# A fixed order on every engine for blocks 1 to 5 of the first layer, instead of one chosen by a scheduler

## The chip, the cores and the metric

The kernel runs on one core of a Trainium2 chip, in one launch. The metric is the device time of that launch in microseconds (us); lower is better. The profile is one further execution of the same program, taken by the hardware profiler.

The engines are named as the profile names them: PE (TensorE, matmuls; PEld is its weight load), DVE (VectorE), ACT (ScalarE), SP (SyncE, which here only issues DMAs). Each engine takes its instructions in its own written order and waits on semaphores for the others.

## The reference, cut to what matters

Attention over chunks of 32 queries, then two feed-forward layers on 3072 tokens of width 512, each with a hidden width of 2048:

```
for c in range(24):                       # chunk of 32 queries, local keys + 8 memory keys
    scores = scale * q_c @ k_full.T       # 64 keys per chunk
    a = exp(scores - max);  a = a / (sum(a) + 1e-9)
    out[c] = a @ v_full
x = out.transpose(0, 2, 1, 3).reshape(3072, 512)
h = relu(x @ w_in);  x = (h * h) @ w_out            # first layer
h = x @ w2_in;       x = softplus(h) @ w2_out       # second layer
```

## The kernel before, in words

**Blocks and steps.** The first layer goes over the tokens in 6 blocks of 512 (`NB`), and in each block over 16 slices of the hidden width (`f`, `KF`). One slice of one block is a step: `h_mm` makes the slice of the hidden product in a PSUM bank `hp` (12 matmuls), `act1` on ACT applies relu, square and a rounding copy `gh`, `act1_low` on DVE subtracts to get the low half `gl`, and `out_mm` (12 matmuls: low weights by `gh`, high weights by `gh`, high weights by `gl`, for each of the four accumulators `acc0` to `acc3`) adds the slice's share to the block's output. Every product is split into high and low halves so that fp32r matmuls give fp32 accuracy. `out_mm` of a slice runs two steps after its `h_mm` (`LOOK`), and at `f == 0` of the next block the last two are worked off; then `evac` copies the four accumulators to tiles `ev` (even ones on ACT, odd ones on DVE) and stores each to `x2s` in DRAM. `ev` and the relu result `r` share one ring of three buffers (tag `tmp`).

**Attention beside it.** While block n runs, attention for block n+1 is made in four pairs, one each four steps: `p_scores` (64 small matmuls), `p_exp` (on DVE maximum and subtraction, on ACT the exponential), `p_norm` (on DVE sum, reciprocal, multiplication), `p_squares` (16 DVE transposes of 32x32 squares into `pt`), `p_values` (64 small matmuls), `p_out` (two ACT copies to `xf`). At the end of a block `x_split` splits `xf` into `xh` (ACT) and `xl` (DVE). The last block, n = 5, has no attention left.

**Weight preparation.** The second layer's weights arrive as 64-bit floats. Pieces of work (`jobs2`) load them to `cf` tiles, join them to fp32 (`r_conv`: one ACT pass, three DVE passes), form sums (a Strassen-like scheme for the second layer), split them into halves (`halves`: an ACT copy, then a DVE subtraction) and store them to `wa`, `wb`, `wo`. About one piece is written into each step.

**What sets the order.** Block 0 stands in the written order on all engines. From `step(1, 0)` on, PE and SP keep the written order and a scheduler places the instructions of ACT and DVE by its own simulated times. Each engine then keeps that order on the chip, whatever the real times are.

Of the kernel before, what the change touches and what calls it, by code (L numbers as in the profile page):

```python
# [55 lines left out]
def body(ctx: ExitStack, tc: tile.TileContext, qk, vW, w1, w2, out):  # L56
# [132 lines left out]
        p_t[n] = t  # L189


    def p_squares(n):
        t = p_t.pop(n).rearrange("p (a i) (h k) -> p i h a k", i=2, h=2)
        pt = at.tile([P, UC * 2, 2 * PU, CHUNK], F32, tag="pt", name="pt", bufs=1)
        for i in range(2):
            for h in range(2):
                b = (2 * i + h) * 32
                for g in range(UC * 2):
                    nc.vector.transpose(pt[b:b + 32, g], t[g * 32:(g + 1) * 32, i, h])  # L199
        pt_t[n] = pt.rearrange("k (c r) (j u) q -> k c r j u q", c=UC, j=2)  # L200

# [153 lines left out]
    def g_step(n, f, hp, cols=ALL):  # L355
        pending.append((n, f, act1(hp, cols), cols))
# [13 lines left out]
    def store(out, in_):  # L370
        nc.sync.dma_start(out=out.bitcast(F32), in_=in_.bitcast(F32))

    def r_load(k, f, part):
        t = cf_tile(k, (P, DM), I64)
        nc.sync.dma_start(out=t, in_=w2[f][:, part * DM:(part + 1) * DM])
        v = t.bitcast(U32).rearrange("p (n t) -> p n t", t=2)
        return v[:, :, 1], v[:, :, 0]

    def r_conv(f, top, low):
        nc.scalar.activation(out=f, in_=top.bitcast(F32), func=AF.Abs, scale=2.0**-112)  # L380
        nc.vector.tensor_scalar(low, low, 2.0**-29, 7.0, op0=ALU.mult, op1=ALU.min)
        f = f.bitcast(U32)
# [7 lines left out]
    def halves(hi, lo, x):  # L390
        nc.scalar.copy(out=hi, in_=x)  # L391
        nc.vector.tensor_tensor(out=lo, in0=x, in1=hi.bitcast(F32), op=ALU.subtract)  # L392

    def in_jobs(p):
        k0, k1, k2 = 0, 1, 2
        d = {}

        def load(i):
            d["r", i] = r_load((k0, k1)[i], 2 * p + i, 0)

        def conv(i):
            if i == 0:
                d["f"] = cf_tile(k2)
            r_conv(d["f"][:, i], *d["r", i])

        def sums():
            f = d["f"].rearrange("p i (h q) -> p i h q", h=2)
            s = d["s"] = cf_tile(k0, (P, 4, QW))
# [7 lines left out]
            store(wb[p][:, 0:2], split(k1, f[:, :, 1]))  # L416
            t = f[:, 1].bitcast(F32R)
            halves(t[:, 0], t[:, 1], f[:, 0, 0])
            store(wa[p][:, 0], t)

        def split(k, x):
            t = cf_tile(k, (P, 2, 2, QW), F32R)
            halves(t[:, :, 0], t[:, :, 1], x)
            return t

        def last():
            t = split(k1, d["s"][:, 0:2])
            u = split(k2, d["s"][:, 2:4])
            store(wa[p][:, 1:3], t)
            store(wa[p][:, 3:4], u[:, 0:1])  # L430
            store(wb[p][:, 2:3], u[:, 1:2])

        return lambda: load(0), lambda: load(1), lambda: conv(0), lambda: conv(1), sums, last

    def out_jobs(f):
        d = {}

        def load():
            d["r"] = r_load(f % 2, f, 1)

        def conv():
            x = cf_tile(2, (P, DM))
            r_conv(x, *d["r"])
            t = cf_tile(f % 2, (P, 2, DM), F32R)
            halves(t[:, 0], t[:, 1], x)
            store(wo[f // 2][:, f % 2], t)

        return load, conv

    ij, oj = [in_jobs(p) for p in range(KP)], [out_jobs(f) for f in range(KF)]  # L450
    jobs2 = [(0, [ij[0][0], ij[0][1]])]
    for p in range(KP):
        after = ij[p + 1][0:2] if p + 1 < KP else (oj[0][0], oj[1][0])
        jobs2 += [(1, [ij[p][2]]), (1, [ij[p][3]]), (1, [ij[p][4]]), (0, [ij[p][5], after[0]]), (0, [after[1]])]
    for f in range(KF):
        jobs2.append((1, [oj[f][1]]))
        jobs2.append((-1, [oj[f + 2][0]] if f + 2 < KF else []))


    xo = {}  # L460
# [7 lines left out]
    def x_jobs(grp, k):  # L468
        d = {}

        def sums(i):
            b11, b12, b21, b22 = (xf_t[2, grp, k][:, j // 2, j % 2] for j in range(4))
            if i == 0:
                if grp == 0:
                    t = late[0].tile([P, 4, BLK], F32, tag="r2", name="xs")
                    d["t"] = t[:, 0], t[:, 1], t[:, 2]
                else:
                    d["t"] = [tmp("xs") for _ in range(3)]
            t3, t2, t4 = d["t"]
            if i == 0:  # L480
                todo = (t3, b22, b12), (b12, b12, b11)
            else:
                todo = (t2, b22, b12), (t4, b21, t2)
            for o, a, b in todo:
                nc.vector.tensor_tensor(out=o, in0=a, in1=b, op=ALU.subtract)
            d["x"] = b11, b12, t2, b22, b21, t3, t4

        def split(i):
            if k == 0:
                xo[grp, i] = wpool.tile([P, 2, 2, BLK], F32R, tag=f"w{i}", name=f"xo{i}")  # L490
            t = xo[grp, i]
            halves(t[:, 0, k], t[:, 1, k], d["x"][i])

        return [lambda: sums(0), lambda: sums(1)] + [lambda i=i: split(i) for i in range(7)]


    with tc.manual_schedule(engines={mybir.EngineType.SP}):
# [134 lines left out]
        def step(n, f):  # L632
            if f == 0:
                out_step()
            hp = h_mm(1, n, f)
            pair = (n + 1) * PB + f // 4 if n < NB - 1 else -1
            if pair >= 0 and f % 4 == 0:
                if f == 0:
                    p_scores(pair)
                p_exp(pair)  # L640
                later_loads(pair)
            if n == NB - 1 and f == 0:
                at_ctx.__exit__(None, None, None)
                pb_ctx.__exit__(None, None, None)
                pl.append(ctx.enter_context(tc.tile_pool(name="pl", bufs=2, space=bass.MemoryType.PSUM)))
                late.append(ctx.enter_context(tc.tile_pool(name="late", bufs=1)))
            g_step(n, f, hp)
            act1_low()
            if pair >= 0 and f % 4 == 0:
                p_norm(pair)  # L650
                p_squares(pair)
            if jobs2 and not (jobs2[0][0] == 1 and pair >= 0 and f % 4 == 0):
                for job in jobs2.pop(0)[1]:
                    job()
            while jobs2 and jobs2[0][0] == -1 and (n == NB - 1 or f % 2):
                for job in jobs2.pop(0)[1]:
                    job()
# [9 lines left out]
            if f == KF - 1 and n < NB - 1:  # L667
                x_split((1, n + 1))
            if f == 0:
                out_step()  # L670
            while len(pending) > LOOK:
                out_step()
            if pair >= 0 and f in (3, 7, 11, KF - 2):
                (p_values if f == KF - 2 else p_both)(pair)
                p_out(pair)
# [141 lines left out]
                xq.setdefault(f, []).extend(j[:n])  # L817
                j = j[n:]

        with tc.manual_schedule(engines={mybir.EngineType.PE}):  # L820
            for n in range(1, NB):
                for f in range(KF):
                    step(n, f)
            assert not jobs2
            for _ in range(3):
                fetch()
            while pending:
                out_step()
            fetch()
            for grp in range(NGR):  # L830
                second_stage(grp, first_stage(grp))

# [44 lines left out]
```

## Time and profile before

| | |
|---|---|
| runs, median (lowest to highest) | 1137.39 us (1135.9 to 1139.78), 3 runs |
| profiled execution | 1138.33 us, span 1136.6 us |
| PE busy | 1091.1 us, 96% of the span |
| DVE busy | 754.5 us, 66% |
| ACT busy | 586.0 us, 52% |
| mean granted TensorE clock | 0.989 of 2.4 GHz |

The span is the time from the program's first to its last instruction; 1.7 us of the execution's time lie outside it. PE is the engine whose work fills the span, so what counts is the time in which it stands idle or runs at a lower clock; busy time of DVE and ACT counts only where PE waits for it.

### The profile page before, as it was taken

Reading aid. Unit: us, or ns where it says so; the run is one execution under the profiler, and the core shown is the slowest. Engines: PE = TensorE matmul, PEld = TensorE weight load, DVE = VectorE, ACT = ScalarE, POOL = GpSimd, SP = SyncE. Lnnn points to the kernel's source line nnn. Section 1 sums busy time; section 2 is a strip of 40 time slices with the busy share of each in tenths; the row PEclk is TensorE's granted clock in tenths of the full one; section 3 lists DMA queues with packets and bytes.
Section 4 is the critical chain, followed back from the end, with each engine's and each line's share of the span. In section 5 each row is a group of like instructions: output and inputs, shape, how many; then the busy total and the mean of one; then the engine's idle time right before and its main releaser. Section 6 shows DMA issues by size and latency. Waiting matters only on the chain.

```text
span 1136.6 us, 18578 instructions
## 1 busy us (share of the span) xinstructions
PE 1091.1 (96%) x7592; PEld 892.8 (79%) x7592; DVE 754.5 (66%) x1239; ACT 586.0 (52%) x914; POOL 0.7 (0%) x6
## 2 busy tenths in 40 slices
PE   6899989999999899998999999999999999999998
PEld 5668868878888687877887878788888888788887
DVE  6899567656665675766364399954498963599822
ACT  3666534435444434444455477733476742576622
POOL 0000000000000000000000000000000000000000
PEclk9999989999999999999999999999999999999999
DMA  9941154435236234632363555532655432656201
GB/s 367 400 161 45 55 162 151 145 125 175 74 125 217 78 138 143 203 113 93 107 236 93 174 187 204 185 137 75 228 192 212 157 108 97 229 192 219 83 1 74
DMA packets 49428, 174.99 MB, mean 154 GB/s; under 512 B 5312, under 2 KB 5312, under 8 KB 41152
## 3 DMA queue, kind: packets, MB, share of 16 engines
q1 hardware_dynamic: 49344, 173.82, 44.0%
q8 instruction: 59, 0.97, 0.4%
q14 instruction: 25, 0.20, 0.1%
HBM read 138.15 MB, written 35.65 MB: 153 GB/s over the span
## 4 chain that ended last, share of the span: by engine, by line
PE 74%; DVE 10%; DMA 10%; ACT 3%; issue 2%; SPq 1%; DVEq 0%; ACTq 0%
PE bk L799 23%; PE bk L711 18%; PE acc L324 15%; PE hp L288 5%; PE hp L289 5%; PE hp L290 5%; DMA cf<-w 4%; DVE pt L199 3%; DMA wo<-cf 2%; DMA wb<-cf 1%; DMA out<-cf 1%; DMA x2s<-ev 1%; DVE cf L392 1%; PE xs L233 1%; DVE cf L110 1%
## 5 line engine op out<-in xcount | busy, mean ns | idle before, releaser
L324 PE MATMUL acc<-gh,w 128*128 128x512 f32 (+1 forms) x776 | 240.5, 392 | 7.0 <-DVE ev L333 6.4
L799 PE MATMUL bk<-ws,gh 128*128 128x512 f32 x768 | 236.5, 389 | 0.0
L711 PE MATMUL bk<-xo,ws 128*128 128x512 f32 x1008 | 230.5, 390 | 2.5 <-ACT h L750 1.3
L711 PEld LDWEIGHTS bk<-xo,ws 128*128 128x128 f32 x1008 | 188.9, 188 | 43.2 <-ACT h L750 2.1
L324 PEld LDWEIGHTS acc<-gh,w 128*128 128x128 f32 x776 | 144.5, 189 | 37.9 <-DVE ev L333 7.3
L799 PEld LDWEIGHTS bk<-ws,gh 128*128 128x128 f32 x768 | 144.1, 188 | 30.0 <-ACT h L731 0.2
L288 PE MATMUL hp<-xh,w 128*128 128x512 f32 (+1 forms) x388 | 156.6, 404 | 9.8 <-ACT r L300 5.3
L324 PE MATMUL acc<-gl,w 128*128 128x512 f32 (+1 forms) x388 | 152.0, 392 | 7.7 <-DVE gl L309 7.6
L289 PE MATMUL hp<-xl,w 128*128 128x512 f32 (+1 forms) x388 | 153.9, 397 | 0.3 <-DVE xl L264 0.2
L290 PE MATMUL hp<-xh,w 128*128 128x512 f32 (+1 forms) x388 | 153.3, 395 | 0.0
L799 PE MATMUL bk<-ws,gl 128*128 128x512 f32 x384 | 149.5, 389 | 0.0
L392 DVE TENSOR_TENSOR gl<-h,gh 128x512 fp32r<-128x512 f32 x96 | 65.9, 688 | 84.4 <-ACT gh L391 84.1
L391 ACT CAST gh<-h 128x512 fp32r<-128x512 f32 x96 | 59.4, 622 | 112.7 <-PE bk L799 112.3
L309 DVE TENSOR_TENSOR gl<-r,gh 128x512 fp32r<-128x512 f32 (+1 forms) x97 | 65.7, 683 | 57.3 <-ACT gh L303 56.9
L300 ACT ACTIVATE r<-hp 128x512 f32<-128x512 f32 (+1 forms) x97 | 57.0, 588 | 86.9 <-PE hp L290 77.6
L288 PEld LDWEIGHTS hp<-xh,w 128*128 128x128 f32 x388 | 75.2, 194 | 27.6 <-ACT r L300 6.1
L324 PEld LDWEIGHTS acc<-gl,w 128*128 128x128 f32 x388 | 73.3, 189 | 25.7 <-DVE gl L309 10.8
L289 PEld LDWEIGHTS hp<-xl,w 128*128 128x128 f32 x388 | 75.2, 194 | 15.8 <-DVE xl L264 0.5
L290 PEld LDWEIGHTS hp<-xh,w 128*128 128x128 f32 x388 | 75.1, 194 | 15.8
L799 PEld LDWEIGHTS bk<-ws,gl 128*128 128x128 f32 x384 | 72.1, 188 | 14.9
L199 DVE STREAM_TRANSPOSE pt<-t 32x128 f32<-32x128 f32 x256 | 77.5, 303 | 3.7
L717 ACT ACTIVATE cf<-h 128x1024 f32<-128x1024 f32 x48 | 51.0, 1062 | 27.6 <-DVE cf L721 20.1
(82 smaller groups left out, 1145.0 us busy)
## 6 DMA issues: line engine op xcount, KB each, us to landing
ws<-wa SPq DMA_DIRECT2D x24, 1024.0 KB, 4.8
ws<-wo SPq DMA_DIRECT2D x24, 1024.0 KB, 4.8
ws<-wb SPq DMA_DIRECT2D x24, 768.0 KB, 4.2
r<-w SPq DMA_DIRECT2D x16, 1024.0 KB, 11.1
cf<-w SPq DMA_DIRECT2D x32, 512.0 KB, 4.6
qk<-qk SPq DMA_DIRECT2D x46, 336.0 KB, 4.8
v<-vW SPq DMA_DIRECT2D x44, 256.0 KB, 4.4
wo<-cf SPq DMA_DIRECT2D x16, 512.0 KB, 4.4
```

Of the source, the lines that this page charges most:

```text
L199: nc.vector.transpose(pt[b:b + 32, g], t[g * 32:(g + 1) * 32, i, h])
L288: nc.tensor.matmul(out=hp, lhsT=b, rhs=xh[:, c], start=(c == 0), stop=False)
L289: nc.tensor.matmul(out=hp, lhsT=a, rhs=xl[:, c], start=False, stop=False)
L290: nc.tensor.matmul(out=hp, lhsT=a, rhs=xh[:, c], start=False, stop=(c == KD - 1))
L300: nc.scalar.activation(out=r, in_=hp, func=AF.Relu)
L309: nc.vector.tensor_tensor(out=gl, in0=r, in1=gh.bitcast(F32), op=ALU.subtract)
L324: nc.tensor.matmul(out=acc[m][:, cols], lhsT=a, rhs=b, start=(f == 0 and j == 0 and cols.start == 0), stop=(f == KF - 1 and j == 2),)
L391: nc.scalar.copy(out=hi, in_=x)
L392: nc.vector.tensor_tensor(out=lo, in0=x, in1=hi.bitcast(F32), op=ALU.subtract)
L711: nc.tensor.matmul(out=bk, lhsT=a, rhs=b, start=(start and n == 0), stop=(n == 5), skip_group_check=not start)
L717: nc.scalar.activation(out=z, in_=h, func=AF.Abs)
L799: nc.tensor.matmul(out=bk, lhsT=a, rhs=b, start=(f == 0 and j == 0), stop=(f == KF - 1 and j == 2))
```

## The change

From `step(1, 0)` to the end of the first layer all engines keep the written order; the second layer is left as it was (PE and SP written, ACT and DVE by the scheduler). Inside `step` the order is written anew:

- First the low half of the step before (`act1_low`) and the low halves that the pieces left over (`flush`), then `h_mm`.
- Then the loads and ACT's first pass (`starts`) of one piece of weight preparation.
- Then, at every fourth step, the softmax with the first 8 of its 16 transposes; the other 8 stand in the next step. At `f == 0` the softmax stands behind relu and `p_scores`.
- Then relu, square and copy, and at the step's end the piece's DVE work and its splits, whose low halves and stores wait for the next step's `flush`.
- `x_split` stands before the relu of step 15 instead of behind it.
- A piece is now one load, one join, one set of sums or one set of splits, and it is skipped only at `f % 8 == 0`.

```
-    def r_conv(f, top, low):
+    def r_abs(f, top, low):
         nc.scalar.activation(out=f, in_=top.bitcast(F32), func=AF.Abs, scale=2.0**-112)
+
+    def r_join(f, top, low):
+        f = f.bitcast(U32)
         nc.vector.tensor_scalar(low, low, 2.0**-29, 7.0, op0=ALU.mult, op1=ALU.min)
...
+    lows = []
+
+    def low_half(hi, lo, x, *stores):
+        nc.vector.tensor_tensor(out=lo, in0=x, in1=hi.bitcast(F32), op=ALU.subtract)
+        for o, i in stores:
+            store(o, i)
+
+    def halves(hi, lo, x, *stores, late=False):
         nc.scalar.copy(out=hi, in_=x)
-        nc.vector.tensor_tensor(out=lo, in0=x, in1=hi.bitcast(F32), op=ALU.subtract)
+        if late:
+            lows.append(lambda: low_half(hi, lo, x, *stores))
+        else:
+            low_half(hi, lo, x, *stores)
+
+    def flush():
+        while lows:
+            lows.pop(0)()
...
+        return [
+            (False, [at(load, 0)], [], []),
+            (True, [at(load, 1)], [at(start, 0)], [at(join, 0)]),
+            (True, [], [at(start, 1)], [at(join, 1)]),
+            (True, [], [], [sums]),
+            (True, [], [], [last]),
+        ]
...
+    jobs2 = [j for p in range(KP) for j in in_jobs(p)]
+    for f in range(0, KF, 2):
+        a, b = out_jobs(f), out_jobs(f + 1)
+        jobs2 += [(False, [a[0]], [], []), (True, [b[0]], [a[1]], [a[2]]), (True, [], [b[1]], [b[2]])]
...
         def step(n, f):
             if f == 0:
                 out_step()
+            if rest:
+                act1_low()
+            flush()
             hp = h_mm(1, n, f)
+
             pair = (n + 1) * PB + f // 4 if n < NB - 1 else -1
-            if pair >= 0 and f % 4 == 0:
-                if f == 0:
-                    p_scores(pair)
+            work = ()
+            if jobs2 and not (jobs2[0][0] and pair >= 0 and f % 8 == 0):
+                _, loads, starts, work = jobs2.pop(0)
+                for job in (*loads, *starts):
+                    job()
+
+            def softmax():
                 p_exp(pair)
                 later_loads(pair)
+                p_norm(pair)
+                p_squares(pair, 0)
+
+            if pair >= 0 and f % 4 == 0 and f > 0:
+                softmax()
...
+            if f == KF - 1 and n < NB - 1:
+                x_split((1, n + 1))
             g_step(n, f, hp)
-            act1_low()
-            if pair >= 0 and f % 4 == 0:
-                p_norm(pair)
-                p_squares(pair)
...
+            if pair >= 0 and f == 0:
+                p_scores(pair)
+                softmax()
+            if pair >= 0 and f % 4 == 1:
+                p_squares(pair, 1)
+            for job in work:
+                job()
...
-        with tc.manual_schedule(engines={mybir.EngineType.PE}):
+        with tc.manual_schedule():
             for n in range(1, NB):
                 for f in range(KF):
                     step(n, f)
             assert not jobs2
+            act1_low()
+            flush()
...
+        with tc.manual_schedule(engines={mybir.EngineType.PE}):
             for grp in range(NGR):
                 second_stage(grp, first_stage(grp))
```

**Place one: DVE in the first step of block 1.** Before, from the low half `gl` of step (1, 0) to the copy of accumulator 3 (`acc_698`; `acc_696` is accumulator 1, `sc`, `t`, `s` and `pt` are the softmax, `cf` the weight preparation):

```order
L309 TENSOR_TENSOR gl<-r,gh 128x512
L177 TENSOR_TENSOR t<-sc,m 128x512
L333 COPY ev<-acc_696 128x512
L185 TENSOR_REDUCE s<-t 128x8
L186 TENSOR_SCALAR s<-s 128x8
L187 RECIPROCAL s<-s 128x8
L188 TENSOR_TENSOR t<-t,s 128x512
L381 TENSOR_SCALAR cf<-cf 128x512
L199 STREAM_TRANSPOSE pt<-t 32x128 x16
L383 SCALAR_TENSOR_TENSOR cf<-cf 128x512
L381 TENSOR_SCALAR cf<-cf 128x512
L333 COPY ev<-acc_698 128x512
```

In the change, the same stretch of DVE, with the semaphores that each row waits for (DMAHW is the landing of a DMA; the one of the second `ev` row is the store of the first):

```order
L177 TENSOR_TENSOR t<-sc,m 128x512 [waits DVE_49]
L185 TENSOR_REDUCE s<-t 128x8 [waits Activation_49]
L186 TENSOR_SCALAR s<-s 128x8 [waits DVE_49]
L187 RECIPROCAL s<-s 128x8 [waits DVE_49]
L188 TENSOR_TENSOR t<-t,s 128x512 [waits DVE_49]
L202 STREAM_TRANSPOSE pt<-t 32x128 [waits DVE_49]
L202 STREAM_TRANSPOSE pt<-t 32x128 x7
L337 COPY ev<-acc_696 128x512 [waits PE_49]
L337 COPY ev<-acc_698 128x512 [waits DMAHW4_49,DVE_49,PE_49]
L313 TENSOR_TENSOR gl<-r,gh 128x512
L202 STREAM_TRANSPOSE pt<-t 32x128 x8
L388 TENSOR_SCALAR cf<-cf 128x512 [waits DMAHW6_49]
```

The low half `gl` of step (1, 0) moved from ahead of the softmax's subtraction to behind both `ev` copies, the first `ev` copy moved behind 8 transposes, and half of the transposes moved behind all of them. Since `gl` comes later, its `r` holds one of the three `tmp` buffers, and the second DVE copy takes the buffer of the first one. The rows in the first steps of blocks 2, 3 and 4 stand the same way.

**Place two: ACT in steps 3 to 5 of block 3.** Before, up to and with relu, square and copy of step 4 (rows `r<-hp`, `r<-r`, `gh<-r`; L380 is the first pass on a loaded weight, `xf<-xs` is `p_out`, L178 the exponential):

```order
L380 ACTIVATE cf<-cf 128x512 [waits DMAHW6_49,DMAHW7_49,DMAHW0_49,DVE_49]
L380 ACTIVATE cf<-cf 128x512 [waits DMAHW1_49]
L391 CAST cf<-cf 128x2x256 [waits DMAHW5_49,DVE_49,Activation_49]
L391 CAST cf<-cf 128x256 [waits DVE_49]
L249 COPY xf<-xs 128x2x128 [waits PE_49]
L249 COPY xf<-xs 128x2x128
L178 ACTIVATE t<-t 128x512 [waits DVE_49]
L391 CAST cf<-cf 128x2x256 [waits DMAHW6_49,Activation_49]
L391 CAST cf<-cf 128x2x256 [waits DMAHW7_49,Activation_49]
L300 ACTIVATE r<-hp 128x512 [waits PE_49]
L301 ACTIVATE r<-r 128x512 [waits Activation_49]
L303 CAST gh<-r 128x512 [waits Activation_49]
```

In the change, ACT from the casts of step 3 to the relu of step 5:

```order
L404 CAST cf<-cf 128x2x256 [waits DVE_49]
L404 CAST cf<-cf 128x256 [waits DVE_49]
L253 COPY xf<-xs 128x2x128 [waits PE_49]
L253 COPY xf<-xs 128x2x128
L178 ACTIVATE t<-t 128x512 [waits DVE_49]
L304 ACTIVATE r<-hp 128x512 [waits PE_49]
L305 ACTIVATE r<-r 128x512 [waits Activation_49]
L307 CAST gh<-r 128x512 [waits Activation_49]
L404 CAST cf<-cf 128x2x256 [waits DMAHW2_49]
L404 CAST cf<-cf 128x2x256 [waits DMAHW3_49]
L304 ACTIVATE r<-hp 128x512 [waits PE_49]
```

Between the `xf` copies of step 3 and the relu of step 4 now stands the exponential alone; the two first passes on loaded weights moved behind, to steps 6 and 7, and the two casts that wait for a DMA now stand behind step 4's copy and ahead of step 5's relu.

**Place three: DVE in steps 4 and 5 of block 3.** Before, from the softmax of step 4 to the low halves behind it:

```order
L172 MEMSET xs 64x2x2x8
L176 TENSOR_REDUCE m<-xs 128x8
L177 TENSOR_TENSOR t<-xs,m 128x512
L185 TENSOR_REDUCE s<-t 128x8
L186 TENSOR_SCALAR s<-s 128x8
L187 RECIPROCAL s<-s 128x8
L392 TENSOR_TENSOR cf<-cf 128x2x256
L188 TENSOR_TENSOR t<-t,s 128x512
L392 TENSOR_TENSOR cf<-cf 128x2x256
L199 STREAM_TRANSPOSE pt<-t 32x128 x16
L309 TENSOR_TENSOR gl<-r,gh 128x512 x4
```

In the change, from the same reduction to the second half of the transposes:

```order
L176 TENSOR_REDUCE m<-xs 128x8
L177 TENSOR_TENSOR t<-xs,m 128x512
L185 TENSOR_REDUCE s<-t 128x8
L186 TENSOR_SCALAR s<-s 128x8
L187 RECIPROCAL s<-s 128x8
L188 TENSOR_TENSOR t<-t,s 128x512
L202 STREAM_TRANSPOSE pt<-t 32x128 x8
L313 TENSOR_TENSOR gl<-r,gh 128x512
L399 TENSOR_TENSOR cf<-cf 128x2x256 x2
L202 STREAM_TRANSPOSE pt<-t 32x128 x8
```

The low half of step 4 now stands behind 8 transposes instead of 16, and one low half stands there instead of four.

## Rows read from the trace of the kernel before

**Rows 1.** One stretch of the span: length, busy us (instructions) by engine, PEclk, DMA share, GB/s.

```profile
140.00:546.00 406.00, 387.14 (x3506) 314.70 (x3499) 263.94 (x600) 183.24 (x332) 0.00 (x0) 0.98 0.42 137
```

**Rows 2.** What PE waited for between 140 and 560 us: total, times, longest.

```profile
PE acc L324 <- DVE ev L333: 6.4, 2, 5.1
PE hp L288 <- ACT r L300: 5.3, 2, 3.7
PE acc L324 <- DVE gl L309: 4.3, 3, 2.0
PE xp L233 <- DVE pt L199: 1.5, 1, 1.5
PE hp L288 <- ACT xh L263: 1.0, 1, 1.0
```

**Rows 3.** Stretches of 5 us behind stalls, columns as in rows 1.

```profile
45.00:50.00 5.00, 3.54 (x11) 2.84 (x12) 4.46 (x6) 4.67 (x7) 0.00 (x0) 0.77 1.04 428
...
155.00:160.00 5.00, 4.40 (x10) 3.48 (x11) 4.97 (x10) 0.62 (x1) 0.00 (x0) 0.50 0.14 52
...
375.00:380.00 5.00, 4.57 (x13) 3.68 (x14) 4.86 (x14) 3.37 (x6) 0.00 (x0) 0.66 0.00 0
535.00:540.00 5.00, 4.50 (x66) 3.78 (x67) 2.62 (x7) 0.65 (x2) 0.00 (x0) 0.58 0.00 0
540.00:545.00 5.00, 5.00 (x18) 4.01 (x17) 0.82 (x2) 1.96 (x4) 0.00 (x0) 0.73 0.00 0
```

**Rows 4.** Timeline of PE, two stalls: start, us, instruction [idle before <-releaser].

```profile
46.46 0.50 PE L288 MATMUL hp<-xh,w 128*128 128x512 f32 x1 [3.07 <-ACT pt L214]
...
382.44 0.50 PE L324 MATMUL acc<-gl,w 128*128 128x512 f32 x1 [1.96 <-DVE gl L309]
```

**Rows 5.** Timeline of DVE, first step of block 1.

```profile
148.84 5.05 DVE L199 STREAM_TRANSPOSE pt<-t 32x128 f32<-32x128 f32 x16
...
154.86 0.68 DVE L333 COPY ev<-acc 128x512 f32<-128x512 f32 x1
```

**Rows 6.** Timeline of DVE and ACT, steps 4 to 6 of block 3.

```profile
371.69 0.69 DVE L176 TENSOR_REDUCE m<-xs 128x8 f32<-128x512 f32 x1
...
374.78 0.59 ACT L300 ACTIVATE r<-hp 128x512 f32<-128x512 f32 x1
374.84 0.65 DVE L392 TENSOR_TENSOR cf<-cf 128x512 fp32r<-128x512 f32 x1
...
375.41 0.69 DVE L188 TENSOR_TENSOR t<-t,s 128x512 f32<-128x512 f32 x1
...
376.62 5.05 DVE L199 STREAM_TRANSPOSE pt<-t 32x128 f32<-32x128 f32 x16
...
381.69 1.90 DVE L309 TENSOR_TENSOR gl<-r,gh 128x512 fp32r<-128x512 f32 x3
```

**Rows 7.** Timeline of PE and DVE, first three steps of block 3.

```profile
340.95 0.86 PE L156 MATMUL sc<-qk 64*32 64x64 f32 x64
...
341.84 0.69 DVE L176 TENSOR_REDUCE m<-sc 128x8 f32<-128x512 f32 x1 [4.37 <-PE sc L156]
...
349.04 0.69 DVE L333 COPY ev<-acc 128x512 f32<-128x512 f32 x1 [2.92 <-DMA x2s<-ev]
...
350.48 0.39 PE L324 MATMUL acc<-gl,w 128*128 128x512 f32 x1
```

**Rows 8.** Tile `ev`: its stores, all 24, then the last boundary's four.

```profile
DMA to landing us min/median/max: 2.3/3.9/7.8
...
DMA to landing us min/median/max: 2.4/2.4/3.0
```

**Rows 9.** What ACT waited for, whole span, and one such wait in the timeline.

```profile
ACT cf L380 <- DMA cf<-w: 81.9, 27, 7.2
...
498.66 0.68 ACT L380 ACTIVATE cf<-cf 128x512 f32<-128x512 f32 x1 [6.06 <-DMA cf<-w]
499.24 0.58 ACT L300 ACTIVATE r<-hp 128x512 f32<-128x512 f32 x1
```

More of the change, by code (lines that the diff above doesn't have):

```diff
@@ L189, in p_norm, with p_squares @@
         p_t[n] = t
[L192 to L200, printed above, removed]
+    sq_t = {}
+    def p_squares(n, i):
+        if i == 0:
+            t = p_t.pop(n).rearrange("p (a i) (h k) -> p i h a k", i=2, h=2)
+            sq_t[n] = t, at.tile([P, UC * 2, 2 * PU, CHUNK], F32, tag="pt", name="pt", bufs=1)
+        t, pt = sq_t[n]
+        for h in range(2):
+            b = (2 * i + h) * 32
+            for g in range(UC * 2):
+                nc.vector.transpose(pt[b:b + 32, g], t[g * 32:(g + 1) * 32, i, h])
+        if i == 1:
+            pt_t[n] = sq_t.pop(n)[1].rearrange("k (c r) (j u) q -> k c r j u q", c=UC, j=2)
     def p_transpose(n):
@@ L377, in r_load @@
         return v[:, :, 1], v[:, :, 0]
-    def r_conv(f, top, low):
+    def r_abs(f, top, low):
         nc.scalar.activation(out=f, in_=top.bitcast(F32), func=AF.Abs, scale=2.0**-112)
+    def r_join(f, top, low):
+        f = f.bitcast(U32)
         nc.vector.tensor_scalar(low, low, 2.0**-29, 7.0, op0=ALU.mult, op1=ALU.min)
-        f = f.bitcast(U32)
         nc.vector.scalar_tensor_tensor(
@@ L388, in r_conv, with start, join, split @@
         )
-    def halves(hi, lo, x):
-        nc.scalar.copy(out=hi, in_=x)
-        nc.vector.tensor_tensor(out=lo, in0=x, in1=hi.bitcast(F32), op=ALU.subtract)
+    lows = []
[4 more added lines that the diff above has]
+    def halves(hi, lo, x, *stores, late=False):
+        nc.scalar.copy(out=hi, in_=x)
+        if late:
[5 more added lines that the diff above has]
+            lows.pop(0)()
     def in_jobs(p):
-        k0, k1, k2 = 0, 1, 2
         d = {}
         def load(i):
-            d["r", i] = r_load((k0, k1)[i], 2 * p + i, 0)
-        def conv(i):
+            d["r", i] = r_load(i, 2 * p + i, 0)
+        def start(i):
             if i == 0:
-                d["f"] = cf_tile(k2)
-            r_conv(d["f"][:, i], *d["r", i])
+                d["f"] = cf_tile(2)
+            r_abs(d["f"][:, i], *d["r", i])
+        def join(i):
+            r_join(d["f"][:, i], *d["r", i])
+        def split(k, x, *stores):
+            t = cf_tile(k, (P, 2, 2, QW), F32R)
+            halves(t[:, :, 0], t[:, :, 1], x, *[(o, t[:, i]) for o, i in stores], late=True)
         def sums():
             f = d["f"].rearrange("p i (h q) -> p i h q", h=2)
-            s = d["s"] = cf_tile(k0, (P, 4, QW))
+            s = d["s"] = cf_tile(0, (P, 4, QW))
             for out, a, b, op in (
@@ L415, in sums, with at @@
                 nc.vector.tensor_tensor(out=out, in0=a, in1=b, op=op)
-            store(wb[p][:, 0:2], split(k1, f[:, :, 1]))
+            split(1, f[:, :, 1], (wb[p][:, 0:2], slice(0, 2)))
             t = f[:, 1].bitcast(F32R)
[L418 to L424, printed above, removed]
-        def last():
[L427 to L433, printed above, removed]
+            halves(t[:, 0], t[:, 1], f[:, 0, 0], (wa[p][:, 0], t), late=True)
+        def last():
+            split(1, d["s"][:, 0:2], (wa[p][:, 1:3], slice(0, 2)))
+            split(2, d["s"][:, 2:4], (wa[p][:, 3:4], slice(0, 1)), (wb[p][:, 2:3], slice(1, 2)))
+        def at(fn, *a):
+            return lambda: fn(*a)
+        return [
[5 more added lines that the diff above has]
+        ]
     def out_jobs(f):
@@ L439, in load, with start, join @@
             d["r"] = r_load(f % 2, f, 1)
-        def conv():
-            x = cf_tile(2, (P, DM))
-            r_conv(x, *d["r"])
-            t = cf_tile(f % 2, (P, 2, DM), F32R)
[L445 to L457, printed above, removed]
+        def start():
+            d["x"] = cf_tile(2, (P, DM))
+            r_abs(d["x"], *d["r"])
+        def join():
+            r_join(d["x"], *d["r"])
+            t = cf_tile(f % 2, (P, 2, DM), F32R)
+            halves(t[:, 0], t[:, 1], d["x"], (wo[f // 2][:, f % 2], t), late=True)
+        return load, start, join
+    jobs2 = [j for p in range(KP) for j in in_jobs(p)]
+    for f in range(0, KF, 2):
+        a, b = out_jobs(f), out_jobs(f + 1)
+        jobs2 += [(False, [a[0]], [], []), (True, [b[0]], [a[1]], [a[2]]), (True, [], [b[1]], [b[2]])]
     xo = {}
@@ L491, in split @@
             t = xo[grp, i]
-            halves(t[:, 0, k], t[:, 1, k], d["x"][i])
+            halves(t[:, 0, k], t[:, 1, k], d["x"][i], late=(grp == 0))
         return [lambda: sums(0), lambda: sums(1)] + [lambda i=i: split(i) for i in range(7)]
@@ L646, in step @@
                 late.append(ctx.enter_context(tc.tile_pool(name="late", bufs=1)))
+            if f == KF - 1 and n < NB - 1:
+                x_split((1, n + 1))
             g_step(n, f, hp)
-            act1_low()
-            if pair >= 0 and f % 4 == 0:
-                p_norm(pair)
-                p_squares(pair)
[L652 to L657, printed above, removed]
+            if pair >= 0 and f == 0:
[5 more added lines that the diff above has]
+                job()
             if n == NB - 1:
@@ L666, in step @@
                     job()
-            if f == KF - 1 and n < NB - 1:
-                x_split((1, n + 1))
             if f == 0:
```

## The prediction

> **What bounds the kernel now.** I read the windows first: in which stretch does PE lose time? From 140 to 546 us, blocks 1 to 5 of the first layer up to the end of block 4, PE is busy 387.1 of 406 us [rows 1]; this is the stretch that the change reorders. Then the waits of PE inside it [rows 2]: 18.5 us in nine waits (6.4 + 5.3 + 4.3 + 1.5 + 1.0). The reader should see that nothing there is a DMA: PE waits for DVE and ACT, which are busy only 264 and 183 of the 406 us [rows 1]. They have room; what is wrong is what stands in front of the awaited instruction.
>
> The timelines show it. At the first step of block 1, DVE does 16 transposes for 5.05 us from 148.84 and only then, behind two more weight passes, the copy of accumulator 3 at 154.86 [rows 5]; PE needs that bank and stands for 5.1 us, the longest wait [rows 2]. In block 3 the relu of step 4 starts on ACT at 374.78 [rows 6], behind the weight passes and casts that the order puts ahead of it, and PE waits 3.7 us for its PSUM bank [rows 2]; then the transposes run from 376.62 and three low halves only from 381.69 [rows 6], so PE waits a further 1.96 us at 382.44 [rows 4].
>
> Last the clock. Three of the stalls are followed by a granted clock of 0.50, 0.66, 0.58 and 0.73 over 5 us [rows 3], stretches in which the engine ran partly at the lower of its two levels (1.2 instead of 2.4 GHz). Lost there: 4.40 x 0.50 = 2.2; 4.57 x 0.34 = 1.6; 4.50 x 0.42 = 1.9; 5.00 x 0.27 = 1.3; together 7.0 us. So the order of ACT and DVE costs **18.5 + 7.0 = 25.5 us** in this stretch, the most that the change can give.
>
> **The change part by part.** No instruction of weight is added or removed; the same passes, transposes and DMAs run. So the sum is made of waits.
>
> *Middle of a block (steps 1 to 15).* Here I follow the queue by durations. A step is 24 matmuls. From the end of `sc` at 341.8 to the `gl` matmul at 350.48 stand 38 matmuls (12 of `out_mm`, 24 of two `h_mm`, 2 more) in 8.7 us [rows 7], 0.23 us each, so 5.5 us a step. The low half of step f is needed when `out_mm` reaches its third matmul two steps on: 2 x 5.5 + 2.7 + 0.5 = 14.2 us after step f began. At the worst DVE has in a softmax step of the new order: a low half and two left-over ones, 2.1; the softmax up to its multiplication, 3.8 (371.69 to 376.10 less 0.6 for the pass at 374.84 [rows 6], with the exponential inside); 8 transposes, half of 5.05, 2.5; a join of three passes, about 1.9 at 0.43 to 0.69 each. That is 10.3, and then the low half, 0.7: done at 11.0, 3 us before it is needed. The next step adds 0.7 + 2.5 + 1.9 = 5.1, under its 5.5, so it catches up. On ACT the exponential and at most one first pass stand before the relu; a PSUM bank of `hp` is needed again two steps later, so the relu may come 8 us after its matmuls ended. I cost the middle at nothing, 1 us for what I overlook. Its cover is those 3 us on DVE; beyond it each us late is a us of PE. The middle's old waits go: all but the two for `ev` [rows 2].
>
> *First step of blocks 1 to 4.* Here the new order makes a wait. DVE now does: reduction as soon as `p_scores` ends, multiplication ended 3.8 us later, 8 transposes 2.5, the copy of accumulator 1 0.7; then the copy of accumulator 3, which reuses the first copy's buffer and so waits until its store has landed; and only behind it the low half of step 0, 0.7, for which PE's third matmul of the step's `out_mm` waits. For block 3 by the old clock times: 341.84 + 3.8 + 2.5 + 0.7 = 348.9; landing L; + 0.1 + 0.7 + 0.7 = 350.4 + L. PE wants it at 350.48 [rows 7]. **The stall is the landing time of one 256 KB store, within 0.2 us.** Queued behind the waiting copy are that low half, the other 8 transposes, the join and the low half of step 1; the last is ready about 5.1 us after the first one and wanted 5.4 us after it (10 matmuls, 12 of `h_mm`, 2 more), so no second stall follows, barely. ACT waits likewise for the first even copy's store, but its next relu is needed later.
>
> What is L? Stores of `ev` landed in 2.3 to 7.8 us, median 3.9, and in 2.4 to 3.0 at the last boundary, where hardly anything else moved [rows 8]. The new one is issued 7 us after the attention loads of the step, and in block 3 the first store, issued among them, had landed by 349.0 [rows 7]. So it is nearest to the quiet rows: I take 2.6. The Trainium skill (DMA: Bandwidth & Descriptors, Anatomy of one DMA) gives a DMA a fixed part of about 2.0 us plus its bytes at 436 GB/s, measured on another issue path: by it, as an estimate, 2.6 us whatever the hour, and 4 x 2.6 us of stall; the median row above would make it 4 x 3.9.
>
> The clock after such a stall: none lost after 1.96 us [rows 4]; after 3.07 us at 46.46 [rows 4] the stretch to 50 us has 0.77, some 3.54 x 0.23 = 0.8, and 0.5 or so beyond. For 2.6 I take 0.8, bounds 0 and 1.5. **Price: 3.4 us each, 13.6 for four**; bounds 4 x 2.3 = 9.2 and 4 x (3.9 + 1.9) = 23. The first step of block 5 has no softmax ahead of the copies; its low half is ready some 2 us early, at no cost. The second layer keeps its order; nothing there.
>
> *Sum.* 25.5 - 13.6 - 1.0 = 10.9 us gained against the profiled execution's 1138.33 (span 1136.6 and 1.7 around it): 1127.4. That execution lay 0.9 above the median of the runs, so against the median 1137.39 - 10.9 = **1126.5 us**, 1.0% less. With the bounds 9.2 and 23 the likeliest case runs from 1122 to 1136, most of it below 1131.
>
> **The rivals.**
>
> *Slower: the store lands late.* One mechanism, at four places: each boundary stall is L and pulls the clock down as after the 5.1 us stall, 2.2 us [rows 3]. For it speaks that the step issues four attention loads, a weight load and in blocks 2 and 3 a piece's stores shortly before, and that stores among such traffic took up to 7.8 us [rows 8]; against it that the deciding store is issued some 7 us later. It decides from L + 2.2 = (25.5 - 1) / 4 = 6.1, L = 3.9: the median of all stores. At L = 5, 4 x 7.2 = 28.8, 1141.7 us.
>
> *Loads in the way: half the gain.* The first pass on a loaded weight stands ahead of exponential and relu, and waits of ACT for those loads were 27 with 81.9 us, up to 7.2 [rows 9]; at 498.66 one waited 6.06 us with the relu right behind it [rows 9]. If such a wait falls on a softmax step it pushes the exponential and all DVE work behind it by more than the 3 us of cover: about 3 us lost at, say, two of them, 1132.5. That ACT and DVE cannot pass a waiting instruction is also what the Trainium skill says (Perfetto Trace Analysis, Per-instruction lifecycle): strict FIFO. Against it: the load is now issued one to two steps, 5 to 11 us, ahead.
>
> *The boundary costs nothing.* If the store lands and is passed on sooner than I think, or PE itself arrives later, all 25.5 us are gained: 1112. Against it: no store of `ev` landed under 2.3 us [rows 8].
>
> *Nothing comes of it*, because the waits only change places: within 1134 to 1140.8, a sum of the first two rivals in their mild form.
>
> **How the numbers follow.** The likeliest case 0.62 (1122 to 1131, most likely 1126.5), loads in the way 0.14, slower 0.10, nothing 0.07, free boundaries 0.07. Leaving out the tops of the slower case and the free boundaries the range is 1118 to 1138. About 0.3%, 3.4 us, is what a measurement of this kernel can tell from no change. Faster than that: 0.62 less a little for its upper bound, 0.09 of the loads, 0.07: 0.75. Within: 0.14. Slower: 0.11.
>
> **What would show it.** Right: in the changed kernel PE has no wait for `ACT r` and none for DVE's `pt` in blocks 1 to 4; four waits of 2.3 to 3.0 us for a low half, each in the third step of a block at the first `gl` matmul of `acc0`; ahead of each, DVE's second `ev` copy with an idle time ended by DMA `x2s<-ev`; granted clock 0.8 or more in the 5 us behind. Busy sums of DVE and ACT as before. Wrong: waits at those places over 4 us with a clock near 0.5 behind them (the slower rival); waits of PE for `ACT r` or `DVE gl` in steps 4 to 14 with ACT's first pass idle on `cf<-w` ahead (loads in the way); or no wait at the third steps.

## The result, and the profile after

The changed kernel took **1122.40 us** (median of 4 runs, 1119.32 to 1124.83) against 1136.64 us of the kernel before on the same chip: ratio 0.9876, 95% interval 0.9834 to 0.9918. It is 1.2% faster; 1126.5 was forecast. The profiled execution took 1124.83 us, its span 1123.1 us.

The windows of the changed kernel, the first the stretch of [rows 1] with the same columns, the second block 5:

```profile
140.00:546.00 406.00, 396.70 (x3622) 324.25 (x3621) 279.60 (x615) 194.96 (x345) 0.00 (x0) 0.99 0.43 146
546.00:640.00 94.00, 94.00 (x417) 77.82 (x416) 36.97 (x56) 45.70 (x76) 0.00 (x0) 1.00 0.39 131
```

PE stands for 9.3 of the 406 us instead of 18.9. The view of PE's waits from 130 to 640 us, which answers to [rows 2], has one row left:

```profile
PE acc L328 <- DVE gl L313: 9.3, 4, 2.4
```

The waits for relu (`ACT r`), for `pt`, for `xh` and for the copies `ev` are gone; four waits for a low half have come. The timeline of PE has them at the third steps of blocks 1 to 4, each at the first matmul on `gl`:

```profile
153.24 0.50 PE L328 MATMUL acc<-gl,w 128*128 128x512 f32 x1 [2.45 <-DVE gl L313]
253.07 0.62 PE L328 MATMUL acc<-gl,w 128*128 128x512 f32 x1 [2.31 <-DVE gl L313]
352.72 0.50 PE L328 MATMUL acc<-gl,w 128*128 128x512 f32 x1 [2.12 <-DVE gl L313]
451.08 0.65 PE L328 MATMUL acc<-gl,w 128*128 128x512 f32 x1 [2.43 <-DVE gl L313]
```

What is late there, the timeline of DVE shows, at the place of [rows 5]:

```profile
145.26 0.69 DVE L188 TENSOR_TENSOR t<-t,s 128x512 f32<-128x512 f32 x1
145.99 2.50 DVE L202 STREAM_TRANSPOSE pt<-t 32x128 f32<-32x128 f32 x8
148.52 0.69 DVE L337 COPY ev<-acc 128x512 f32<-128x512 f32 x1
151.77 0.69 DVE L337 COPY ev<-acc 128x512 f32<-128x512 f32 x1 [2.55 <-DMA x2s<-ev]
152.49 0.69 DVE L313 TENSOR_TENSOR gl<-r,gh 128x512 fp32r<-128x512 f32 x1
```

DVE stands still for 2.55 us, until a store has landed; behind the waiting copy stands the low half that PE wants. From the end of the first copy to the start of the second it is 2.56, 2.23, 2.23 and 2.54 us in the four blocks. The windows behind the stalls, as in [rows 3], those below 0.95:

```profile
150.00:155.00 5.00, 2.55 (x10) 1.81 (x9) 3.10 (x8) 1.85 (x3) 0.00 (x0) 0.93 0.67 215
155.00:160.00 5.00, 5.00 (x18) 3.93 (x17) 4.67 (x10) 2.43 (x4) 0.00 (x0) 0.73 0.17 47
250.00:255.00 5.00, 2.69 (x9) 1.84 (x8) 3.26 (x9) 2.83 (x5) 0.00 (x0) 0.83 0.68 224
255.00:260.00 5.00, 5.00 (x19) 4.03 (x19) 4.69 (x10) 2.59 (x5) 0.00 (x0) 0.83 0.14 38
450.00:455.00 5.00, 3.92 (x10) 3.11 (x11) 4.67 (x13) 1.85 (x3) 0.00 (x0) 0.66 0.15 54
```

PE's busy time in each, times what the clock lacks: 0.2 + 1.35 + 0.5 + 0.85 + 1.3 = 4.2 us. So 9.3 + 4.2 = 13.5 us are still lost, against 25.5 in the prediction's count of the kernel before: 12.0 us gained in this stretch.

### The profile page after: what moved, and what is told of

It is laid out like the page before. It is cut to its first block, busy times and chain, and to the rows that moved or that the text cites. A ratio compares the mean times of both kernels' runs of the same rounds, so it can differ in the third digit from the quotient of the medians.

```text
span 1123.1 us, 18576 instructions
## 1 busy us (share of the span) xinstructions
PE 1088.1 (97%) x7592; PEld 893.1 (80%) x7592; DVE 761.0 (68%) x1239; ACT 589.8 (53%) x914; POOL 0.7 (0%) x6
## 4 chain that ended last, share of the span: by engine, by line
PE 88%; DVE 6%; DMA 2%; ACT 2%; issue 1%; SPq 0%; DVEq 0%; ACTq 0%
PE bk L833 23%; PE acc L328 22%; PE bk L745 18%; PE hp L292 7%; PE hp L293 7%; PE hp L294 7%; PE xs L237 1%; DMA out<-cf 1%; DVE pt L202 1%; PE xs L156 1%; DMA x2s<-ev 1%; DVE cf L110 1%; DVE cf L107 1%; PE sc L156 1%; PE xp L237 1%
## 5 line engine op out<-in xcount | busy, mean ns | idle before, releaser
L328 PE MATMUL acc<-gh,w 128*128 128x512 f32 (+1 forms) x776 | 243.1, 395 | 0.9 <-DVE w L122 0.9
L328 PEld LDWEIGHTS acc<-gh,w 128*128 128x128 f32 x776 | 146.8, 191 | 31.8 <-DVE w L122 1.3
L292 PE MATMUL hp<-xh,w 128*128 128x512 f32 (+1 forms) x388 | 154.8, 399 | 3.5 <-ACT pt L218 3.1
L294 PE MATMUL hp<-xh,w 128*128 128x512 f32 (+1 forms) x388 | 152.0, 392 | 0.0
L328 PEld LDWEIGHTS acc<-gl,w 128*128 128x128 f32 x388 | 74.2, 191 | 29.8 <-DVE gl L313 14.5
```

Source lines behind the costliest of these rows:

```text
L292: nc.tensor.matmul(out=hp, lhsT=b, rhs=xh[:, c], start=(c == 0), stop=False)
L294: nc.tensor.matmul(out=hp, lhsT=a, rhs=xh[:, c], start=False, stop=(c == KD - 1))
L328: nc.tensor.matmul(out=acc[m][:, cols], lhsT=a, rhs=b, start=(f == 0 and j == 0 and cols.start == 0), stop=(f == KF - 1 and j == 2),)
```

## The experiments

Each was timed in rounds beside the kernel before; ratios below 1 are faster than that. "Lost" is worked out for each run as above: PE's idle time from 130 us to the end of the first layer, plus busy time times the lacking clock over windows of 5 us. By that count the kernel before lost 27.0 us there and the changed one 13.5.

**1. The low half ahead of the copies.** In `step`, based on the changed kernel:

```
             if f == 0:
+                act1_low()
                 out_step()
```

> The changed kernel with one line more: at the first step of a block the low half of step 0 stands ahead of the four copies of accumulators instead of behind them. Theory (the landing of a store): the four waits of PE for a low half (2.45, 2.31, 2.12, 2.43 us, 9.3 in all) are the time in which DVE's second copy waits for the store of the first; with the low half ahead of that copy they go, and with them the some 4.2 us of lower clock behind them: 13.5 us less than the changed kernel, about 1109 us, and PE has no wait for a low half in blocks 1 to 4. The low half of step 1 has 0.5 to 2.1 us in hand now, and DVE comes to it earlier by about as much as PE. Rival (the work of DVE in that step, softmax and transposes, is what is late): the low half still comes behind all of these, and waits of 1.5 us or more stay at the third steps; gain under 4 us. Second rival (the wait moves on): PE then waits for the bank of accumulator 3, or at the fourth step, for as long; no gain.

Measured: **1107.94 us** (5 runs), ratio 0.9727 (0.9700 to 0.9754). DVE at the same place, then PE's waits from 140 to 546 us:

```profile
143.49 2.50 DVE L202 STREAM_TRANSPOSE pt<-t 32x128 f32<-32x128 f32 x8
146.01 0.69 DVE L313 TENSOR_TENSOR gl<-r,gh 128x512 fp32r<-128x512 f32 x1
146.62 1.28 DVE L337 COPY ev<-acc 128x512 f32<-128x512 f32 x2
...
PE hp L292 <- ACT r L304: 0.3, 1, 0.3
```

The two copies now follow each other without a wait: with `r` read, its buffer is free, and the ring reaches round. The waits and the lower clock are gone (0.3 us lost), and the time falls by the 13.5 us that the theory gives, 14.5 between the medians. But this moves the low half and frees a buffer in one edit; the next run parts the two.

**2. Another buffer, the same order.**

```
-            e = tmp("ev")
+            e = tmp("ev") if m < 3 else sb.tile([P, BLK], F32R, tag="gl", name="ev", bufs=3).bitcast(F32)
```

> The changed kernel, in which only the copy of accumulator 3 takes its buffer from the ring of the low halves, where one is free, and not from the ring of the other copies; the order of every engine stays through the first layer. Theory (the landing of a store, and nothing of the order by itself): DVE's second copy waits for no store, so the low half of step 0 is ready 2.6 us sooner, at about the time at which PE wants it: the four waits fall from 9.3 us to 0.5 each or less, the clock behind them stays, 1109 to 1113 us. Rival (the low half stands too far back on DVE, whatever it waits for): the order is the same, so the four waits stay at 2 us or more and the time at 1120 or more.

Measured: **1107.81 us** (4 runs), ratio 0.9729 (0.9692 to 0.9767). The low half stands where it stood, behind both copies:

```profile
145.87 1.29 DVE L337 COPY ev<-acc 128x512 f32<-128x512 f32 x2
147.19 0.69 DVE L313 TENSOR_TENSOR gl<-r,gh 128x512 fp32r<-128x512 f32 x1
...
PE acc L328 <- DVE gl L313: 0.4, 1, 0.4
```

So it was the landing of the store, and not the place of the low half on DVE. The time is below the 1109 to 1113 us expected, because the lower clock went with the waits: no window of 5 us between 130 and 640 us is below full clock.

**3. All 16 transposes in the softmax step.** `p_squares(pair, 1)` right behind `p_squares(pair, 0)`, none in the next step.

> The changed kernel with all 16 transposes in the softmax step again, none in the next step: 2.5 us more of DVE in each softmax step. Theory (a chain at the boundary, cover in the middle): at the first steps of blocks 1 to 4 the stall grows by those 2.5 us, from 9.3 to about 19 in all, with a clock behind it as behind the 5.1 us stall of the kernel before, 2.2 us each instead of 1: about 14 us more; in the middle the low halves have 4 to 6 us in hand at nearly all softmax steps and nothing shows, but for step 4 of block 4, which has 1.1 us in hand and gives a wait of about 1.4. Together 16 us: about 1138 us. Rival (middle steps have no room): waits for a low half at many of steps 4, 8 and 12 too, and 1145 us or more. Rival (the store decides alone, whenever it starts): boundary stalls as they were, about 1123 us.

Measured: 1136.10 us (10 runs), ratio 0.9984 (0.9968 to 1.0000). PE's waits from 130 to 640 us:

```profile
PE acc L328 <- DVE gl L313: 19.6, 4, 5.0
```

At the boundary the chain adds up: 9.3 + 4 x 2.5 = 19.3, 19.6 measured, and 8.4 us of clock instead of 4.2. In the middle PE waits nowhere, and the time in hand (from the end of a low half to PE's first matmul on it) falls by about those 2.5 us, from 6.2 to 3.7 at step 4 of block 2. Step 4 of block 4, where a wait of 1.4 had been expected, has 1.8 in hand: a load that DVE waits for ahead of it cost 4.0 us in the changed kernel and 2.7 here. This one edit takes back nearly all of the gain.

**4 and 5. What is the gain: a fixed order, or the new one?** Run 4 fixes the old order (`manual_schedule()` for all engines in the kernel before), run 5 leaves ACT and DVE of the new one to the scheduler (`manual_schedule(engines={PE})` in the changed kernel).

> The kernel before, with its own written order kept on ACT and DVE too through blocks 1 to 5, no scheduler there. It tells apart what the change consists of: fixing any order, or the new one. Theory A (the new order makes the gain): in the old written order the low half stands right behind relu, square and copy, 16 transposes behind it, and a whole piece of weight preparation with its own ACT and DVE turns and a wait for its load behind that; PE waits at several middle steps and at the first steps for accumulator 3: 1132 us or more, the gain of the change not had. Theory B (the scheduler was the trouble, any sensible fixed order does): 1118 to 1128, as the changed kernel or better, since in this order the low half of step 0 stands ahead of the copies and the four waits for it can't arise.

> The changed kernel, with its new written order for PE and SP, but ACT and DVE placed by the scheduler in blocks 1 to 5 as before. Theory A (the new written order makes the gain, whoever places ACT and DVE): 1118 to 1128 us. Theory B (the scheduler's order is the trouble): weight passes stand ahead of relu and low halves again, PE waits for relu and transposes in middle steps come back, 1130 to 1145 us.

Measured: **old order, fixed: 1151.19 us** (4 runs), ratio 1.0102 (1.0069 to 1.0135); **new order, scheduler: 1114.08 us** (4 runs), ratio 0.9777 (0.9749 to 0.9805). PE's waits, 130 to 640 us, of the one and of the other:

```profile
PE acc L324 <- DVE ev L333: 22.8, 6, 4.6
PE acc L324 <- DVE gl L309: 4.8, 1, 4.8
PE hp L289 <- DVE xl L264: 1.5, 2, 1.2
...
PE acc L328 <- DVE gl L313: 3.1, 1, 3.1
```

Both theories A hold by the times, run 5 with more gain than was expected; but of the waits at middle steps that A expected of the fixed old order only one came, 4.8 us in block 5. Medians, in us:

| written order | ACT and DVE by the scheduler | fixed |
|---|---|---|
| old | 1136 to 1139 (the kernel before) | 1151.2 (run 4) |
| new | 1114.1 (run 5) | 1122.4 (the change) |
| new, low half ahead of the copies | 1113.2 (run 7) | 1107.9 (run 1) |

Fixing an order makes the kernel slower by 1.0% with the old one (38.3 us lost) and by 8 us with the new one; only with the low half ahead of the copies is fixed the faster (run 7). The new order as the scheduler's input makes the whole gain and more. In the fixed old order the boundary is again what costs, by the copies this time. Four of the six waits come from copies behind 16 transposes; the other two, 4.28 and 4.29 us in blocks 2 and 5, from a copy that waits for a store, 6.52 and 7.18 us on DVE. The first of these two, and DVE in the first step of block 1 of run 5:

```profile
262.88 0.69 DVE L333 COPY ev<-acc 128x512 f32<-128x512 f32 x1 [6.52 <-DMA x2s<-ev]
...
138.81 0.69 DVE L313 TENSOR_TENSOR gl<-r,gh 128x512 fp32r<-128x512 f32 x1 [0.46 <-ACT gh L307]
...
143.68 0.69 DVE L337 COPY ev<-acc 128x512 f32<-128x512 f32 x1 [1.75 <-DMA x2s<-ev]
```

In run 5 the copy waits for the store too, but the scheduler has put the low half ahead of it, and PE does not wait there. That is why run 5 is faster than the change. The waits for relu, `pt` and `xh` that the kernel before has (7.8 us) are not in run 4, which has 1.5 us for `xl` instead, and not in run 6: it was the scheduler's placing of the old written order that made them.

**6. The old order fixed, its copies ahead of the transposes.** In `step` the second `out_step()` of `f == 0` moves from the end to right behind `act1_low()`.

> The old written order fixed on all engines (old_fixed), with one thing moved: at the first step of a block the last product of the block before and the copies of its accumulators are written right behind the low half of step 0, ahead of sum, multiplication, 16 transposes and the piece of weight preparation. In old_fixed PE waited 22.8 us in six waits for the copy of an accumulator and 4.8 and 1.5 besides. Theory (in a fixed order only the boundary costs; in the middle the old order has room as well): the six waits go, with them 6 to 8 us of lower clock: 1116 to 1126 us, though nothing of the new order of the middle is there. Rival (the middle of the old order is too tight): waits for low halves, transposes or relu come up at middle steps as soon as PE arrives earlier, 1135 us or more.

Measured: 1123.34 us (4 runs), ratio 0.9889 (0.9861 to 0.9916), as the changed kernel. The six waits for copies are gone. Five of 1.0 to 3.9 us for low halves (9.0) are left, four of them at the fourth step of a block, behind the 16 transposes, and the longest in block 5, where DVE waits 6.3 us for an input of the second layer; besides these, three for `xl` (1.8). So nothing of the new order of the middle is needed for a gain of this size, given a fixed order and a good boundary.

**7. The new order, low half ahead, by the scheduler** (edits 1 and 5 together).

> The order of low_first as written, but ACT and DVE placed by the scheduler in blocks 1 to 5, as before the change. Theory (fixing the order is worth nothing by itself, only what the order makes PE wait for): PE is busy 405.7 of 406 us in low_first and can't gain; the scheduler, which took the new written order to 1114 us with one wait of 3.1 for a low half, has that wait taken away: 1106 to 1112 us, the same as low_first. Rival (a fixed order is needed): the scheduler moves weight passes ahead again, and waits of PE of 3 us and more come in, 1114 or more.

Measured: 1113.15 us (4 runs), ratio 0.9781 (0.9736 to 0.9825). Neither as expected: it is as run 5, where the scheduler had the low half ahead of the copies already, and the wait of 3.1 us stays, with two of 0.7 and 0.3 beside it. The long one is at 510 us, a middle step of block 4, not at the boundary as I had taken it: in run 5 ACT and DVE stand there for a load (`cf<-w`, 5.0 and 4.2 us) just ahead of the softmax. Once the boundary is mended, the fixed order is 5.2 us better than the scheduler's by the medians, 3 of them this wait; the intervals overlap a little, so a gain from fixing by itself is likely, but not shown clear of noise.

**8. No late low halves of the weights.** `late = False` as first line of `halves`.

> The changed kernel, in which the low half of each weight split is subtracted at once, right behind its copy on ACT, and stored in the same step, instead of at the beginning of the next step. Theory (the middle has 4 to 6 us in hand, so this part of the order is worth nothing): DVE waits some 0.6 to 1 us for each of ACT's copies in a step's splits, which the time in hand covers: 1119 to 1126 us, as the changed kernel, and the four waits at the first steps as there. Rival (the deferral is what makes the middle free): waits of PE for low halves or transposes in middle steps, 1128 us or more.

Measured: 1122.93 us (4 runs), ratio 0.9868 (0.9830 to 0.9907), as the changed kernel; three waits of 0.7 to 1.2 us come in addition, between 453 and 546 us. This part of the new order is worth at most these. What the smaller pieces or the place of `x_split` are worth by themselves was not tried.

**9. 5 us more of DVE in the middle.** On run 1; `p_again` repeats the transposes of both halves:

```
             if pair >= 0 and f % 4 == 0 and f > 0:
                 softmax()
+                for again in (0, 1):
+                    p_again(pair, again)
```

> The kernel with the low half ahead of the copies (low_first), in which the softmax steps 4, 8 and 12 of each block do 16 transposes a second time besides, work without use: 5.0 us more of DVE at 12 places. It measures the cover of the middle. By the prediction's count the cover there is 3 us: waits of PE of 2 us at 12 places, 24 us and some clock, 1132 us or more. By the low halves of low_first, read at each step against PE's first matmul on them, 4.2 to 6.2 us are in hand at all but one of these places: about 0.8 us at each of the four steps 12 and at one step 8, nothing at the other steps 4 and 8, but 2 to 4.5 at step 4 of block 4, which has 0.3 in hand: 6 to 9 us in all, 1114 to 1118 us.

Measured: 1157.47 us (4 runs), ratio 1.0180 (1.0131 to 1.0229): far above the 1114 to 1118 us of the count by time in hand, and not by the 2 us at 12 places of the other. Step 4 held as expected (4.5 us in block 4, next to nothing in the others). Step 8 lost 1.8, 1.8 and 2.1 us in blocks 1 to 3, where about 1 us should have stayed in hand; why was not traced. Step 12 lost 6.3 to 7.0 us in each of blocks 1 to 3 and 4.3 in block 4. Step 8 and step 12 of block 1 on PE, then ACT, DVE and SP's load ahead of step 12:

```profile
198.67 0.50 PE L335 MATMUL acc<-gl,w 128*128 128x512 f32 x1 [1.81 <-DVE gl L320]
229.75 0.80 PE L335 MATMUL acc<-gl,w 128*128 128x512 f32 x1 [6.89 <-DVE gl L320]
...
216.36 0.66 ACT L391 ACTIVATE cf<-cf 128x512 f32<-128x512 f32 x1 [5.89 <-DMA cf<-w]
216.93 0.62 ACT L178 ACTIVATE t<-t 128x512 f32<-128x512 f32 x1
...
217.58 0.69 DVE L185 TENSOR_REDUCE s<-t 128x8 f32<-128x512 f32 x1 [5.31 <-ACT t L178]
...
210.75 1.55 SPq L386 DMA_DIRECT2D cf<-w  x2
```

In run 1 the same loads were issued earlier, and ACT's first pass did not wait (SP and ACT of low_first):

```profile
201.12 1.31 SPq L379 DMA_DIRECT2D cf<-w  x2
...
206.38 0.67 ACT L384 ACTIVATE cf<-cf 128x512 f32<-128x512 f32 x1
```

The loads stand on SP behind the stores of the step before, these wait for DVE's late low halves, ACT's first pass waits for the load, the exponential stands behind it, and DVE waits for the exponential. DVE's delay comes back to DVE.

**10. The same, with the exponential ahead of the waiting pass.** On run 9; the piece's `starts` move from ahead of the softmax to behind `g_step`.

> The kernel with 16 needless transposes at steps 4, 8 and 12 (more_dve5), in which ACT's first pass on a loaded weight stands behind relu, square and copy, no longer ahead of the exponential. In more_dve5 the waits came at step 12: 6.9 us, where the load was issued 9.6 us later than in low_first, behind stores that wait for DVE's late low halves, and ACT's first pass stood 5.9 us for it with the exponential behind. Theory (a loop: DVE late, stores late, load late, exponential late, DVE later still): with the exponential ahead of the waiting pass the waits at the four steps 12 fall from 6.3 to 7.0 us to some 2 each, what is left of the added 5.0 us with three passes of a join ahead of the low half, and step 4 of block 4 falls below 3; 10 to 15 us in all, 1118 to 1128 us against 1157. Rival (5 us are simply too much for DVE, loads have no part): the waits stay at 5 us and more at steps 12, 1145 us or more.

Measured: 1139.53 us (10 runs), ratio 1.0018 (1.0002 to 1.0035). The waits at the four steps 12 fell to 2.40, 2.31, 2.38 and 2.12 us, as the loop demands; the first, and PE's waits from 130 to 660 us:

```profile
227.02 0.50 PE L335 MATMUL acc<-gl,w 128*128 128x512 f32 x1 [2.40 <-DVE gl L320]
...
PE acc L335 <- DVE gl L320: 19.9, 12, 5.5
```

The total missed the range: step 4 of block 4 kept 5.5 us, where I had expected under 3 (there DVE itself waits for a load, 3.8 us, in a join that stands ahead of the softmax), steps 8 of blocks 1 to 3 kept 1.0 to 1.3 each, four of 0.4 to 0.5 came in at the fourth steps, and 7.5 us of clock went with the waits. So the loop made the greater part of the waits at step 12 (24.4 us fell to 9.2), but the time lies in neither range.

## Why the prediction was right, by its own steps

- **What can be gained, 25.5 us:** right. With the four stalls away as well (run 1) 0.3 us is lost in the first layer from 130 us on, and the median is 30.7 us below that of the kernel before beside it; 26.7 of these are from the count over 130 us to the end of the layer (27.0 before), the other 4 I have not traced to a place.
- **Middle of a block, 1 us:** 0 measured. The old waits for relu, `pt` and low halves are all gone. The cover was mis-sized: 3 us forecast. The changed kernel at step 4 of block 2, DVE's low half and PE's first matmul on it:

```profile
271.80 0.69 DVE L313 TENSOR_TENSOR gl<-r,gh 128x512 fp32r<-128x512 f32 x1
...
278.67 0.39 PE L328 MATMUL acc<-gl,w 128*128 128x512 f32 x1
```

  271.80 + 0.69 to 278.67 is 6.2 us in hand; read in the same way, step 12 of that block has 4.4 and step 4 of block 4 only 1.1. It can be spent by addition only in part: 2.5 us came off it one for one (run 3), but run 9 took 5.0 of it and lost up to 7 at a step.
- **First steps of blocks 1 to 4, the landing of one store:** right in mechanism (runs 1 and 2) and size: 2.6 each forecast, 2.45, 2.31, 2.12 and 2.43 measured, four times where the argument put them. The Trainium skill (DMA: Bandwidth & Descriptors, Anatomy of one DMA) gives, as an estimate by its fixed part and rate for another issue path, 2.6 us for such a store; the 2.23 to 2.56 us between the two copies lie up to 0.4 us below that.
- **The clock behind them:** 0.8 each forecast, 4.2 in all measured, by far not alike: none behind 2.12 us, 1.3 to 1.6 behind the others, the upper end of the bounds. Waits and clock together are 13.5 us, forecast 13.6, and that they meet so closely is luck: the waits came out 1.1 us under their term, the clock 1.0 us over its own. In run 8 the same four waits (9.3 us) came with 1.2 us of clock.
- **Second low half, in time "barely":** 2.1 us in hand in three blocks and 0.5 in block 3, against 0.3; no stall. Block 3 is the one that kept its full clock, so its 0.5 is what the sum describes; in the others PE ran at the lower clock and came later.
- **Block 5 and the second layer:** no cost; PE is busy all 94 us of block 5's window. At its first step 0.85 us were in hand instead of some 2.
- **The sum:** 10.9 us forecast against the profiled execution, 13.5 measured, 14.2 between the medians. Of the 2.6 missing, 1.1 is in this stretch (12.0 instead of 10.9): 1.0 from the middle, 0.1 from the boundary. The rest is outside the terms and within what runs scatter: before 130 us, where the change does nothing, the profiled execution of the changed kernel lost 26.7 us by the same count and that of the kernel before 22.4, so single executions differ by some 4 us there.
- **The rivals.** *The store lands late* did not come: all four under 2.6. *The boundary costs nothing* is what runs 1 and 2 build: 1108 us. *Loads in the way* was hidden rather than absent: in the changed kernel ACT still stood for loads 14 times, 43.0 us in all, between 140 and 560 us (22 times, 71.3 us before), but the middle had more in hand than I thought; it came forth in runs 5, 7 and 9. *Nothing comes of it* is out: its 1134 us lie above every run of the changed kernel.

Where the prediction's words fell short: it spoke of "the order of ACT and DVE" as the cost, and that is what it was, but it did not ask whether fixing it helps. Fixed, the old order is slower than the scheduler's, and so is the new one as long as its low half stands behind the copies.

## What to carry to other kernels

Where an engine keeps its order, look for the instruction in front of the awaited one that waits for a DMA: a copy into a ring of buffers waits for the store of an earlier one, and everything behind it waits too. Read what frees the ring's buffers; here one line that reads the old buffer first, or one buffer from another ring, was worth as much as the whole reordering. And time in hand on one engine is no sum to be spent when its results go through a store queue to a load that the same engine's next work depends on: 2.5 us more were free in the middle here, 5.0 were not.

## What was unexpected of the hardware

How long PE stalls does not by itself say whether the clock falls behind it, for stalls of 2 to 3 us. In the changed kernel 2.12 us at 352.72 were followed by a full granted clock, while 2.31 and 2.43 us at 253.07 and 451.08 were followed by windows at 0.83 and 0.66, partly at 1.2 GHz. In run 8 it is the other way round; its stalls at 150.65 and 347.05 and the windows that hold them:

```profile
150.65 0.50 PE L328 MATMUL acc<-gl,w 128*128 128x512 f32 x1 [2.46 <-DVE gl L313]
150.00:155.00 5.00, 4.35 (x19) 3.58 (x20) 4.70 (x12) 2.57 (x5) 0.00 (x0) 1.00 0.54 157
...
347.05 0.52 PE L328 MATMUL acc<-gl,w 128*128 128x512 f32 x1 [2.14 <-DVE gl L313]
345.00:350.00 5.00, 2.95 (x8) 2.35 (x9) 4.23 (x11) 2.13 (x4) 0.00 (x0) 0.74 0.62 202
```

And the stall of 3.11 us that runs 5 and 7 have at the same step cost 1.5 us of clock in run 5 and none in run 7. What decided it was not tried. Under the larger stalls of run 9 the loss was 12.6 us on 34.8 us of waits, about a third again: in these runs a PE wait of over 2 us mostly cost more than itself.
